# Windowed attention and an MLP on one core: the first block turned in 64-column halves, and the second product done plainly in place of seven half-size products

## The chip, the cores and the metric

The kernel runs on one core of a Trainium2 chip. A core has a matrix engine (TensorE, PE in the profile; its weight loads are PEld), a vector engine (VectorE, DVE), an activation engine (ScalarE, ACT), a general one (GpSimd, POOL) and a sync engine (SyncE, SP) that here only issues transfers. They run side by side, each through its own queue of instructions in order, and wait for each other by semaphores. The metric is the device time of one execution in microseconds. All arithmetic on PE is in 16-bit floats with 32-bit sums.

## The reference

Attention over a window of 128 tokens and 4 sink tokens, for 4 batches of 8 heads, 768 tokens and 64 numbers a head; its result, heads side by side (3072 tokens x 512), goes through an MLP.

```python
scores = scale * np.matmul(q, k.transpose(0, 1, 3, 2))
is_sink = pos[None, :] < int(n_sink)                    # n_sink = 4
rel = pos[:, None] - pos[None, :]
in_window = (rel >= 0) & (rel < int(window))            # window = 128
scores = np.where(is_sink | in_window, scores, -1000000000.0)
a = np.exp(scores - np.max(scores, axis=-1, keepdims=True))
a = a / (np.sum(a, axis=-1, keepdims=True) + 1e-09)
x = np.matmul(a, v)                                     # -> (3072, 512)
h = x @ w_in                                            # w_in 512 x 2048
g = h * (1.0 / (1.0 + np.exp(-1.702 * h)))
out = g @ w_out                                         # w_out 2048 x 512
```

## The kernel before

The tokens are cut into 12 blocks of 256, three to a batch. Each block goes through these stages:

- `load`: q, k and v come in as 32-bit floats by DMA. Blocks 0 to 3 bring q and k in two halves each, in rows of 2 KB (8 tokens of a head); later blocks bring them whole in shorter rows. They are cast to 16 bits (L295 is the helper `copy` that every cast and plain copy goes through): for block 0 on DVE or ACT, for block 1 on POOL, DVE or ACT, from block 2 on by POOL.
- `turn`: q and k are turned so that a head's 64 numbers lie across partitions (`blkT`). Blocks 0 to 3 are turned on PE (`turn_on_pe`, L541: four 128 x 128 products with a permutation matrix `perm` for each of q and k and each of two sets of tokens, and one or two copies out of PSUM); later ones by a transposing DMA (`turn_by_dma`, L563).
- `scores`: four head pairs a block; scores of a pair against the block and the block before it (L613), sinks (L593); in blocks 0 and 1 the mask is added by PE (L605), later it is multiplied in after the exponential by DVE (L645). ACT makes the exponentials (L638, L625).
- `back`: the attention product (L678), whose extra column gives the sum; its reciprocal (L696) and the normalisation, on DVE (L700) or, from block 3 on, ACT (L704); then a turn to `xT`, on PE for blocks 0 to 2 (L724), by DMA later (L712).
- `mm1`: the first MLP product, 64 products of 256 columns a block (L751), in eight groups; ACT makes a tanh of each group (L763) and DVE the gated activation `gT` (L765), since g is h(tanh(0.851 h) + 1)/2.
- the second product. Blocks 0, 1 and 11 do it plainly (`mm2`, L780): two groups of 16 products of 512 columns, each summed in a PSUM bank, halved and copied out by ACT (L797). Blocks 2 to 10 do it by `mm2_by_seven` (L870): a 2 x 2 split of tokens and of output and inner columns, with seven half-size products in place of eight: 56 products of 256 columns a block. For this DVE (or POOL) makes four forms of the weights once (`forms_of_w`, L825), DVE makes four sums and differences of the activations for each block (`forms_of_g`, L846, 144 instructions of 256 elements), ACT takes intermediate sums out of PSUM (L897, L900, L902) and DVE joins them (L903, L908). Three of the weight forms lie in the memory of the third load buffer (`third`).

PSUM has 8 banks. The order of all work is made before the kernel runs: `Plan.run` takes operations with their dependences, planned durations, priorities, the limits on banks ("o" is the class of the second product) and, for some, a choice of engines, and lays down one order for each engine's queue. So any change of an operation can move many others. The sizes of the rings of buffers stand in one line:

```python
RS, RQ, RV, RA, RX, RG, RTH, RO = 3, 2, 4, 4, 3, globals().get('OPT',{}).get('RG',3), 3, 2
```

RS counts the load buffers, RA the exponentials `at`, RG the activations `gT`, RO the output buffers (here two rows of 512 wide). Weights come by POOL's DMA queue (L376); the first waits for the last of block 1's four q and k loads. PE runs products with zeros (L982) while it has nothing to do at the start.

Of the kernel before, what the change touches and what calls it, by code (L numbers as in the profile page):

```python
# [14 lines left out]
P = 128  # L15
# [187 lines left out]
def kernel(  # L203
# [25 lines left out]
    KT, KX, AHEAD = globals().get('OPT',{}).get('KT',4), 3, globals().get('OPT',{}).get('AHEAD',0)  # L229
    RB, KM = 4, globals().get('OPT',{}).get('KM',2)  # L230
    RS, RQ, RV, RA, RX, RG, RTH, RO = 3, 2, 4, 4, 3, globals().get('OPT',{}).get('RG',3), 3, 2
    KS, LASTS = globals().get('OPT',{}).get('KS',2), globals().get('OPT',{}).get('LASTS',NK-1)
# [13 lines left out]
    perm = pool.tile([P, P], FP16, name="perm")  # L246
    dummy = pool.tile([P, 8], FP16, name="dummy")
# [7 lines left out]
    third = pool.tile([P, 3 * H * 2 * D], FP32, name="third")  # L255
    qk32 = ring("qk32", RS - 1, (P, 2, H, 2, D), FP32)
    v32 = ring("v32", RS - 1, (P, H, 2, D), FP32)
    qk32.append(third[:, 0 : 2 * H * 2 * D].rearrange("p (e h i d) -> p e h i d", e=2, h=H, i=2))
    v32.append(third[:, 2 * H * 2 * D :].rearrange("p (h i d) -> p h i d", h=H, i=2))
    wf = [third[:, 1024 * n : 1024 * n + 1024].bitcast(FP16).rearrange("p (s c) -> p s c", s=NS) for n in range(3)]  # L260
    wf += ring("wf", 1, (P, NS, d_model // 2), FP16)
    gF = ring("gF", 2, (P, NS, 3, P), FP16)
    part = pool.tile([P, 1024], FP32, name="part")
# [10 lines left out]
    osb = ring("osb", RO, (P, 2 * d_model), FP32)  # L274
    bank = [psp.tile([P, 512], FP32, name=f"bank{i}") for i in range(8)]

    OPT_ = globals().get("OPT", {}).get
    plan = Plan(8, {"m": 1, "s": 5, "t": 4, "a": 2, "x": 2, "h": RTH, "o": OPT_("NO", 3)})
# [32 lines left out]
    OPT = globals().get("OPT", {})  # L311
    VS_AT = NEVER + 14.505
# [17 lines left out]
    def masks():  # L330
# [9 lines left out]
        out=perm.rearrange("r (h g) -> r h g", h=NP), in_=ident.rearrange("r (g h) -> r h g", h=NP)),  # L340
        [o_ident], prio=NEVER, kind="const")

# [18 lines left out]
    OPT = globals().get("OPT", {})  # L361
    CAST_QK = ["DVE ACT", "POOL DVE"] + ["POOL"] * (NK - 2)
# [35 lines left out]

    o_cqk, o_cv, o_vs = {}, {}, {}
    o_qkT, o_ks, o_se, o_m, o_xT = {}, {}, {}, {}, {}  # L400

    def load(k):
        b, r = divmod(k, R)
        sl = k if k < RS else (k - 1) % (RS - 1)
# [5 lines left out]
        for e, src in enumerate((q, k_ap)):  # L410
            eng, dma = ("ACT", nc.scalar) if k == 0 and e else ("POOL", nc.gpsimd) if k == 2 else ("SP", nc.sync)
            lq[e] = []
            if k < KT:
# [28 lines left out]
        war = reuse("qk16", k % RQ)  # L442
        if k >= KT:
            C = slots(c16)
            for e in range(2):
                for j in range(2):
                    for i in range(2):
                        def f(eng, e=e, j=j, i=i):
                            copy(eng, C[64 * i : 64 * i + 64, e, :, j].rearrange("s p (h d) -> s p h d", h=2),
                                 dst[64 * j : 64 * j + 64, e, :, i].rearrange("s (p h) d -> s p h d", h=2))  # L450
                        o = plan.any(cast(512, CAST_QK[k]), f, lq[e] + war, prio=nominal(k - 1, -7), kind="cqk")
                        o_cqk[k, 2 * e + j, i] = o
        else:
# [8 lines left out]
        for o in {id(x): x for (kk, _, _), x in o_cqk.items() if kk == k}.values():  # L462
            uses("s32", sl, o)
# [41 lines left out]
    def turn(k):  # L505
# [7 lines left out]
        if k < KT:  # L513
# [5 lines left out]
        for p in range(NP):  # L519
            o_qkT[k, p] = [o[p] for o in o_t]  # L520
# [14 lines left out]

    def turn_on_pe(k, e, i, T, C, war):
        base = attend(k, 0) - 5 * L / 8

        def tp():
            for a in range(4):  # L540
                nc.tensor.transpose(f16(o_tp)[:, bass.ts(a, P)], C[:, a].rearrange("s h d -> s (h d)"), perm)  # L541

        o_tp = op("PE", 4 * pe_ns(P), 3 * pe_ns(P) + P / 2.4 + 166, tp, [o_cqk[k, e, 0], o_cqk[k, e, 1], o_perm],
# [112 lines left out]
    def back(k, p):  # L656
# [41 lines left out]
        def normal(eng):  # L698
            if eng == "DVE":
                nc.vector.tensor_tensor(out=X, in0=avp()[:, :, :, 0:D], in1=rc.to_broadcast((P, 2, 2, D)), op=ALU.mult)  # L700
                return
            for j in range(2):
                for i in range(2):
                    nc.scalar.activation(out=X[:, j, i], in_=avp()[:, j, i, 0:D], func=AF.Copy, scale=rc[:, j, i : i + 1])  # L704

        o_n = plan.any({"DVE": (340, 430), **({"ACT": (430, 550)} if OPT_("XA", 3) <= k else {})}, normal,
# [28 lines left out]
    o_g = {}  # L735

# [32 lines left out]
    def mm2(k):  # L769
        b, r = divmod(k, R)  # L770
        g = gT[k % RG]
        for j, c0, c1 in ((0, 0, 512), (1, 0, 512)) if k < NK - 1 else ((0, 0, 512), (1, 0, 384), (1, 384, 512)):
# [17 lines left out]
            if not c0:  # L790
                war = reuse("osb", (k % RO, j))
            O = osb[k % RO][:, bass.ts(j, d_model)]
# [12 lines left out]
            for i in range(2):  # L805
# [6 lines left out]
                uses("osb", (k % RO, j), o_d)  # L812

    def forms_of_w():

        W = w_out16.rearrange("p (s e) (h c) -> p s e h c", e=2, h=2)
        free = [o for (kk, _, _), o in o_cqk.items() if kk == 2] + [o for p in range(NP) for o in o_cv[2, p]]
        for j in range(4):
            x = slice(2 * j, 2 * j + 2)
            b11, b12, b21, b22 = (W[:, x, e, h] for e in range(2) for h in range(2))  # L820
            t1, t2, t3, t4 = (wf[n][:, x] for n in range(4))
            for n, (o_, a, b_, what) in enumerate(((t1, b12, b11, ALU.subtract), (t2, b22, t1, ALU.subtract),
                                                   (t3, b22, b12, ALU.subtract), (t4, b21, t2, ALU.subtract))):
                def f(eng, o_=o_, a=a, b_=b_, what=what):
                    (nc.gpsimd if eng == "POOL" else nc.vector).tensor_tensor(out=o_, in0=a, in1=b_, op=what)  # L825
                deps = [o_w[4 + j]] + ([o_wf[j, n - 1]] if n in (1, 3) else [])
                if n == 3:
                    deps.append(o_wf[j, 1])
                o_wf[j, n] = plan.any({"POOL": (1110, 1250), "DVE": (450, 550)}, f, deps + (free if n < 3 else []),
                                      prio=nominal(KS + 1, OPT_("WFP", -9) + j), kind="wf")  # L830

    def forms_of_g(k):

        g, F = gT[k % RG], gF[k % 2]
        G = g.rearrange("p (s e) (t q) -> p s (e t) q", e=2, t=2)
        war = reuse("gF", k % 2)
        w = OPT_("GW", 2)
        for s in range(0, NS, w):
            x = slice(s, s + w)
            a11, a21, a12, a22 = (G[:, x, n] for n in range(4))  # L840
            s1, s2, s4 = (F[:, x, n] for n in range(3))
            last = [o_g[k, i] for i in range(s, s + w)] + war
            four = []
            for o_, a, b_, what in ((s1, a21, a22, ALU.add), (s2, s1, a11, ALU.subtract), (a21, a11, a21, ALU.subtract), (s4, a12, s2, ALU.subtract)):
                def f(eng, o_=o_, a=a, b_=b_, what=what):
                    (nc.gpsimd if eng == "POOL" else nc.vector).tensor_tensor(out=o_, in0=a, in1=b_, op=what)  # L846
# [187 lines left out]
```

## Time and profile before

| | us |
|---|---|
| median of 3 runs | 223.22 (222.3 to 223.94) |
| the profiled execution | 222.3 |
| its span | 220.4 |
| PE busy | 209.2 (95%) |
| DVE busy | 177.0 (80%) |
| ACT busy | 135.7 (62%) |
| POOL busy | 93.3 (42%) |
| first MLP product starts | 18.98 |
| last product ends | 216.95 |

The span runs from the first to the last instruction; about 1.9 us lie around it. A product's booked time includes the way through the array, so that products overlap in the profile: how fast they go is read from one start to the next. The granted clock of PE is 1.0 throughout. A line of a group gives the line of the code, engine, operation, what is written from what, shapes, count, busy time and the mean of one in ns, and the idle time of the engine before it with what ended it. In a timeline the first two numbers are start and length in us.

### The profile page before, as it was taken

How to read it: one execution, taken by the hardware profiler on the slowest of the kernel's cores; microseconds unless marked ns; L12 is line 12 of the kernel's file. 1: busy time of each engine (PE TensorE's matmuls, PEld its weight loads, DVE VectorE, ACT ScalarE, POOL GpSimd, SP SyncE). 2: the span in 40 equal slices, each digit the busy share in tenths (PEclk: the TensorE clock that was granted, in tenths of full speed). 3: DMA queues.
4: the chain of work that ended last, by engine and by line, in shares of the span. 5: the costliest groups of instructions: out<-in, count | busy, mean ns of one | idle time of the engine just before them, and what ended most of it. 6: DMA issues, size and time to landing. Idle time of an engine off the chain costs nothing.

```text
span 220.4 us, 5881 instructions
## 1 busy us (share of the span) xinstructions
PE 209.2 (95%) x2282; PEld 164.8 (75%) x2282; DVE 177.0 (80%) x437; ACT 135.7 (62%) x298; POOL 93.3 (42%) x152
## 2 busy tenths in 40 slices
PE   7989999996998999999989999999999999999993
PEld 2447877574766887888878877888888988988852
DVE  3677855399999799889799999999799979875520
ACT  2697645877464777866845745866755656635420
POOL 2495440789995393076390492292840000000000
PEclk9999999999999999999999999999999999999999
DMA  5999999999457909695959939939746024024043
GB/s 192 340 235 205 207 302 234 302 308 287 110 111 143 265 24 190 173 218 104 303 141 194 261 72 175 261 85 236 234 94 147 0 51 100 0 51 95 0 97 97
DMA packets 65916, 36.60 MB, mean 166 GB/s; under 512 B 27968, under 2 KB 61120, under 8 KB 65888
## 3 DMA queue, kind: packets, MB, share of 16 engines
q1 hardware_dynamic: 60848, 30.19, 55.1%
q0 software_dynamic: 4592, 5.37, 12.8%
q10 hardware_dynamic: 448, 0.66, 0.9%
q8 instruction: 18, 0.29, 0.6%
q14 instruction: 10, 0.08, 0.1%
HBM read 27.56 MB, written 6.29 MB: 154 GB/s over the span
## 4 chain that ended last, share of the span: by engine, by line
PE 65%; DVE 24%; ACT 7%; issue 3%; DVEq 0%; ACTq 0%
PE bank L751 26%; PE bank L870 18%; DVE gT L765 7%; PE bank L780 6%; DVE gF L846 5%; PE bank L678 5%; PE bank L613 4%; ACT at L638 3%; PE bank L982 3%; DVE third L825 2%; DVE at L645 2%; DVE gT L846 2%; ACT th L763 2%; PE bank L605 1%; DVE osb L903 1%
## 5 line engine op out<-in xcount | busy, mean ns | idle before, releaser
L751 PE MATMUL bank<-xT,w_in 128*128 128x256 f16 x768 | 99.4, 273 | 0.2 <-DVE gT L765 0.2
L763 ACT ACTIVATE th<-bank 128x512 f16<-128x512 f32 x96 | 57.8, 604 | 49.1 <-PE bank L751 47.8
L751 PEld LDWEIGHTS <-w_in 128*128 128x128 f16 x768 | 72.7, 98 | 11.2 <-issue 1.8
L765 DVE SCALAR_TENSOR_TENSOR gT<-th,bank 128x512 f16<-128x512 f16 x96 | 65.2, 679 | 17.1 <-ACT th L763 16.4
L295 POOL CAST qk<-qk 64x512 f16<-64x512 f32 (+1 forms) x70 | 44.1, 633 | 39.7 <-DMA qk<-in_q_dram 29.1
L638 ACT ACTIVATE at<-bank 128x512 f16<-128x512 f32 (+1 forms) x96 | 49.1, 577 | 10.1 <-PE bank L613 10.1
L870 PE MATMUL bank<-third,gF 128*128 128x256 f16 x144 | 34.4, 273 | 1.4 <-DVE gF L846 1.4
L870 PE MATMUL bank<-w_out,gT 128*128 128x256 f16 x144 | 34.3, 273 | 0.0
L870 PEld LDWEIGHTS <-gT 128*128 128x128 f16 x288 | 27.7, 98 | 4.1 <-issue 0.9
L645 DVE TENSOR_TENSOR at<-at,bank 128x1024 f16<-128x1024 f16 (+1 forms) x40 | 25.2, 636 | 4.4 <-ACT at L638 4.4
L295 POOL CAST v<-v 64x512 f16<-64x512 f32 (+1 forms) x38 | 24.1, 636 | 2.8 <-PE bank L751 0.9
L870 PEld LDWEIGHTS <-gF 128*128 128x128 f16 x216 | 20.7, 98 | 4.7 <-DVE gF L846 1.9
L678 PE MATMUL bank<-v,at 128*128 128x65 f16 x352 | 21.1, 193 | 2.9 <-DVE at L645 2.4
L780 PE MATMUL bank<-w_out,gT 128*128 128x512 f16 (+2 forms) x112 | 23.6, 349 | 0.0
L678 PEld LDWEIGHTS <-at 128*128 128x128 f16 x352 | 17.1, 97 | 5.6 <-DVE at L645 4.3
L870 PE MATMUL bank<-wf,gT 128*128 128x256 f16 x72 | 17.2, 273 | 0.0
L870 PE MATMUL bank<-w_out,gF 128*128 128x256 f16 x72 | 17.1, 272 | 0.0
L780 PEld LDWEIGHTS <-gT 128*128 128x128 f16 x112 | 9.8, 98 | 7.0 <-issue 0.3
L678 PE MATMUL bank<-vs,ats 128*128 128x65 f16 x128 | 14.8, 193 | 0.0
L846 DVE TENSOR_TENSOR gF<-gF,gT 128x256 f16<-128x256 f16 x36 | 13.8, 382 | 0.8
L613 PEld LDWEIGHTS <-blkT 64*128 64x128 f16 x256 | 8.1, 94 | 8.0 <-issue 6.5
L704 ACT ACTIVATE xb<-bank,rcp 128x64 f16<-128x64 f32 x44 | 10.3, 323 | 5.5 <-DVE rcp L696 5.5
(67 smaller groups left out, 226.7 us busy)
## 6 DMA issues: line engine op xcount, KB each, us to landing
out_dram<-osb SPq DMA_DIRECT2D x46, 128.0 KB, 2.4
v<-in_v_dram SPq DMA_DIRECT2D x11, 512.0 KB, 6.6
qk<-in_q_dram SPq DMA_DIRECT2D x8, 512.0 KB, 4.9
qk<-in_k_dram SPq DMA_DIRECT2D x8, 512.0 KB, 6.1
w_in<-in_moe_w_in_dram POOLq DMA_DIRECT2D x4, 512.0 KB, 9.0
w_out<-in_moe_w_out_dram POOLq DMA_DIRECT2D x4, 512.0 KB, 12.4
qk<-in_q_dram SPq DMA_DIRECT2D x6, 256.0 KB, 5.1
qk<-in_k_dram SPq DMA_DIRECT2D x4, 256.0 KB, 5.2
```

The lines of the kernel that those rows point to most:

```text
L295: {"POOL": nc.gpsimd.tensor_copy, "DVE": nc.vector.tensor_copy, "ACT": nc.scalar.copy}[e](out=out, in_=in_)
L613: nc.tensor.matmul(f32(o_s, 2 * n + i)[:, c : c + w], src[d, j], Q[d].rearrange("d j s -> d (j s)")[:, q0 : q0 + w], start=k >= KM, stop=T ...
L638: nc.scalar.activation(out=A[:, i, 0:W], in_=f32(o_s, 2 * n + i)[:, 0:W], func=AF.Exp, scale=scale)
L645: nc.vector.tensor_tensor(out=A[:, :, 0:W], in0=A[:, :, 0:W], in1=mask(c0, c0 + W).unsqueeze(1).to_broadcast((P, 2, W)), op=ALU.mult,)
L678: nc.tensor.matmul(avp()[:, j, i], a_, v_, start=(n == 0), stop=(n == len(mms) - 1))
L704: nc.scalar.activation(out=X[:, j, i], in_=avp()[:, j, i, 0:D], func=AF.Copy, scale=rc[:, j, i : i + 1])
L751: nc.tensor.matmul(f32(holder[0])[:, bass.ts(e, TB)], w_in16[:, c, bass.ts(Fi, P)], X[:, c] if k < KX else X2[:, :, c], start=(c == 0), st ...
L763: o_t = op("ACT", 477, 600, lambda first=first: nc.scalar.activation(out=th[first.places[0]], in_=f32(first), func=AF.Tanh, scale=0.851), ...
L765: o_g[k, s] = op("DVE", 590, 700, lambda first=first, s=s: nc.vector.scalar_tensor_tensor(out=g[:, 2 * s : 2 * s + 2].rearrange("p a t -> ...
L780: nc.tensor.matmul(f32(holder[0])[:, 0:w], g[:, Fi, bass.ts(j, P)], w_out16[:, Fi, c0:c1], start=(Fi == 0), stop=(Fi == NF - 1),)
L846: (nc.gpsimd if eng == "POOL" else nc.vector).tensor_tensor(out=o_, in0=a, in1=b_, op=what)
L870: nc.tensor.matmul(f32(holder[0])[:, bass.ts(half, N)], lhs, rhs, start=fresh and s == 0 and half == what(0)[0][0], stop=s == NS - 1, skip ...
```

## The change

- Blocks 2 to 10 do the second product by `mm2`, as 0, 1 and 11 did. `mm2_by_seven`, `forms_of_w`, `forms_of_g` and their buffers are gone. The space goes to a third load buffer of its own, to six `at` and five `gT` in place of four and three; the output buffers are three of 512 in place of two of 1024. The second product may hold two banks at once, before three. The normalisation is always DVE's.
- Block 0 loads q and k by halves of head pairs: a half has heads 4y to 4y+3, one after the other, each as 32 rows of 2 KB (before: the even or the odd heads, with heads inside a group of tokens). Number, size and queue of the loads are the same. Each half is cast as it lies and turned by itself in `turn_halves`: for each of eight tokens of a row and each of the two heads of a pair one product of 64 columns into 64 partitions, 64 in all in place of 16 of 128 columns; then two copies. Head pairs 2y and 2y+1 depend on the halves y of q and k only.
- The other blocks that are turned on PE use a second matrix `perm8`, with the old order, which POOL makes after `perm`.
- The first weight load waits for the third of block 1's q and k loads in place of the fourth.

```diff
-    RS, RQ, RV, RA, RX, RG, RTH, RO = 3, 2, 4, 4, 3, globals().get('OPT',{}).get('RG',3), 3, 2
+    KN = globals().get('OPT',{}).get('KN',1)
+    RS, RQ, RV, RA, RX, RG, RTH, RO = 3, 2, 4, 6, 3, 5, 3, 3
...
-    plan = Plan(8, {"m": 1, "s": 5, "t": 4, "a": 2, "x": 2, "h": RTH, "o": OPT_("NO", 3)})
+    plan = Plan(8, {"m": 1, "s": 5, "t": 4, "a": 2, "x": 2, "h": RTH, "o": 2})
...
     o_perm = op("POOL", 330, 450, lambda: nc.gpsimd.tensor_copy(
-        out=perm.rearrange("r (h g) -> r h g", h=NP), in_=ident.rearrange("r (g h) -> r h g", h=NP)),
+        out=perm.rearrange("r (h p g) -> r h p g", h=2, p=2), in_=ident.rearrange("r (p h g) -> r h p g", p=2, h=2)),
         [o_ident], prio=NEVER, kind="const")
+    o_perm8 = op("POOL", 330, 450, lambda: nc.gpsimd.tensor_copy(
+        out=perm8.rearrange("r (h g) -> r h g", h=NP), in_=ident.rearrange("r (g h) -> r h g", h=NP)),
+        [o_ident], prio=NEVER+3, kind="const")
...
+            if k < KN:
+                for y in range(2):
+                    def f(e=e, y=y, src=src, dma=dma):
+                        to = halves(qk16[k % RQ])[:, e, y] if k in CD else dst[:, e].rearrange("s h i d -> s (h i d)")[:, 512 * y : 512 * y + 512]
+                        return dma.dma_start(to, src[b, 4 * y : 4 * y + 4, t0 : t0 + TB].rearrange("h (g i) d -> h g (i d)", i=8))
...
+        if k < KN:
+            for y in range(2):
+                two = [x for e in (1, 0) for x in turn_halves(k, e, y, T, halves(c16)[:, e, y], war)]
+                o_t.append(two)
+                for p in (2 * y, 2 * y + 1):
+                    o_qkT[k, p] = two
+        elif k < KT:
...
+    def turn_halves(k, e, y, T, C, war):
+        base = attend(k, 0) - 5 * L / 8 + 2 * y + e
+
+        def tp():
+            for i in range(8):
+                for h in range(2):
+                    d = slice(64 * h, 64 * h + 64)
+                    nc.tensor.matmul(
+                        f32(o_tp)[d, bass.ts(i, 64)], C[:, bass.ts(i, 64)], perm[:, d], start=True, stop=True,
+                    )
+
+        o_tp = op("PE", TPN, TPN + 170, tp, [o_cqk[k, e, y], o_perm], prio=base, acq=("t", 1), kind="tp")
...
-    def second(k):
-        if KS <= k < LASTS:
-            mm2_by_seven(k)
-        else:
-            mm2(k)
...
         if k_ >= 2:
-            second(k_ - 2)
+            mm2(k_ - 2)
...
-            g = o_first[OPT.get("WG", -1)]
+            g = o_first[OPT.get("WG", -2)]
```

## The prediction

> **What bounds the kernel now.** I read busy time by stretch first, because the shares over the whole span mix the start with the steady part. Columns: PE, PEld, DVE, ACT and POOL busy, clock, DMA share, GB/s.
>
> ```profile
> 20.00:50.00 30.00, 30.00 (x325) 21.70 (x324) 20.08 (x44) 18.75 (x35) 14.26 (x23) 1.00 1.12 266
> 50.00:180.00 130.00, 124.41 (x1428) 103.28 (x1424) 121.34 (x297) 85.08 (x195) 66.81 (x104) 1.00 0.69 163
> 180.00:210.00 30.00, 30.00 (x323) 26.56 (x316) 21.85 (x53) 17.25 (x36) 0.00 (x0) 1.00 0.19 45
> ```
>
> PE has no idle time from 20 to 50 us and from 180 to 210. Between them it idles 130.00 - 124.41 = 5.6 us, exactly where DVE is busy 121.34/130 = 93%. So PE's work sets the length, and the gaps in it are DVE's doing. The waits of PE say it by name:
>
> ```profile
> PE bank L678 <- DVE at L645: 2.4, 3, 1.7
> PE bank L593 <- DVE osb L903: 1.5, 3, 0.7
> PE bank L870 <- DVE gF L846: 1.4, 2, 1.0
> ```
>
> With 0.2 for L751 that is 5.5 us in nine waits. A 256-column matmul is booked for 273 ns, but the next starts 109 ns later, so a wait hides another 0.16: 5.5 + 9 x 0.16 = 7.0 us. What makes them is seen in the timeline at the largest:
>
> ```profile
> 50.33 1.12 DVE L825 TENSOR_TENSOR third<-w_out,third 128x512 f16<-128x512 f16 x1
> 51.37 1.37 DVE L825 TENSOR_TENSOR third<-w_out 128x512 f16<-128x512 f16 x1
> 52.66 0.28 DVE L295 COPY xT<-bank 128x256 f16<-128x256 f16 x1
> 52.86 0.54 DVE L645 TENSOR_TENSOR at<-at,bank 128x768 f16<-128x768 f16 x1
> ```
>
> Two weight forms (L825) stand 2.5 us on DVE ahead of the mask multiply (L645) that the attention product at 53.46 needs. The other two kinds are L846 and L903, DVE steps that exist only for the seven products.
>
> **Part 1, the second product, on the path.** A product of n columns costs its distance to the next start, read from the timeline of PE:
>
> ```profile
> 30.65 1.03 PE L780 MATMUL bank<-w_out,gT 128*128 128x512 f16 x4
> 31.52 1.91 PE L751 MATMUL bank<-xT,w_in 128*128 128x256 f16 x16
> ...
> 98.47 0.27 PE L870 MATMUL bank<-wf,gT 128*128 128x256 f16 x1
> 98.58 0.27 PE L870 MATMUL bank<-w_out,gT 128*128 128x256 f16 x1
> ```
>
> Four of 512 columns take 0.87 us, 217 ns each; 256 columns take 109. Out go 504 matmuls of 256 columns (144 + 144 + 72 + 72 + 72 in the groups), 55.0 us; in come 9 blocks x 32 of 512 columns, 288 x 0.216 = 62.2. Nothing hides this while PE is full: **+7.2 us**.
>
> **Part 2, the engines around it.** DVE loses 144 sums and differences of activations (13.8 + 13.1 + 12.8 + 12.5 = 52.2 us), 18 joins (6.2 + 6.1) and its 13 weight forms (8.7). It takes back 11 normalisations that ACT does now (44 pieces, 10.3 us), each 0.416: 4.6. So DVE goes from 177.0 to 177.0 - 73.2 + 4.6 = 108 us, half the span. ACT loses 12.2 (L897, L900, L902) and those 10.3, and gains 18 copies of 612 ns, 11.0: 135.7 to 124. POOL loses three forms, 3.6. DMA moves the same bytes, and SP's queue carries the same 48 stores and 17 transposes; two stores follow each copy now in place of four after both joins, so what stands behind them in that queue waits no longer than now. All this is beside PE; its worth is only what it does to the 7.0 us of waits. The bounds for these: all go (-7.0), or the same number returns (0). The stretches 20-50 and 180-210, with plain 512-column products or no attention, have DVE at 67-73% and no PE wait; that is the nearest row to a DVE at 50%, so I take nearly all: **-6.3 us**, leaving 0.7 for waits that a new order brings. What is late next: PE cannot lose its 0.1 us steps at changes of work (a score group's first weights, L613, wait 6.5 us in 19 places on "issue"), and those stay as they are. The wider rings (six at, five gT, third load buffers of their own) only take waits away; the plan of instructions holds two banks for the second product in place of three, with one ACT copy as release, and the product after next starts some 8 us later, so I cost it at nothing; were a copy held up by 1 us behind exponentials, it would still be covered.
>
> **Part 3, the start.** Until 18.98 us, where the first block's MLP begins, PE has long gaps and ACT has few:
>
> ```profile
> 7.08 1.56 ACT L295 COPY blkT<-bank 128x256 f16<-128x256 f16 x5 [3.50 <-PE bank L541]
> 9.18 2.50 ACT L638 ACTIVATE at<-bank 128x384 f16<-128x384 f32 x6 [0.54 <-PE bank L613]
> 11.70 1.25 ACT L295 CAST v<-v 64x256 f16<-64x256 f32 x3
> ...
> 14.43 1.88 ACT L295 CAST v<-v 64x512 f16<-64x512 f32 x3
> 16.33 1.09 ACT L638 ACTIVATE at<-bank 128x512 f16<-128x512 f32 x2
> ```
>
> From 9.18 ACT runs almost without a pause until the first tanh at 20.06. The four loads of block 0 keep their queues, their 2 KB rows and their count, so I let them land as now: casts at 4.39, 5.08, 6.12 and 6.79, the last done at 7.22. The gain on paper is that head pairs 0 and 1 need only the first two. But the instruction order of the changed kernel puts all 64 turning matmuls ahead of the first score, so pair 0 waits for the last cast anyway. Sixteen of them cost between 16 x 29 ns = 0.5 us (the attention product's 65 columns, 24 in 0.76) and 16 x 56 = 0.9 (the 128-column turn, 8 in 0.45); the lower is nearer in width. Turned by 7.8 (8.2), masks 0.34, scores 0.3: exponentials could start at 8.5 to 8.9, against 9.18. Then a step stands in ACT's queue that was on DVE: the cast of block 1's first K half.
>
> ```profile
> 8.84 0.43 DVE L295 CAST qk<-qk 128x512 f16<-128x512 f32 x1 [0.30 <-DMA qk<-in_k_dram]
> ```
>
> Its load lands at 8.84 and a cast of this size takes ACT 0.62: the first exponential starts at 9.46, 0.3 **later** than now, with eight exponentials, three V casts and the whole chain queued behind it. Later one V cast of 0.62 moves from ACT to POOL and a 0.3 copy of x comes to ACT: the two cancel. The second permutation (0.29 on POOL, after the first) and the earlier gate of the first weights (block 1's third load in place of its fourth, 0.7 us) lie in POOL's idle 1.8 us before its first cast and 1.0 before L376; uncovered, they would cost 0.3. Bounds of the start: +0.6 if ACT's lead stays lost, -1.0 if the better place of block 0's last two pairs in PE's queue (their attention product comes before two of block 1's score groups) reaches the first MLP product. I take **+0.1**.
>
> The page "TensorEngine Tiling (Array Packing)", section Feature Incompatibilities, speaks against the 64-wide turn: a matmul tiled by columns has no fast weight load. By the page "TensorE: Matmul & The Clock Gate", LDWEIGHTS, 64 columns then take 64/1.2 = 53 ns, so a step would be 0.85 us, an estimate; ACT's wait until 8.84 covers that too, and no row here shows a 64-column load.
>
> The tail (48 products from 209.84 to 216.95, then copies and stores to 220.4) stays.
>
> **Sum.** The profiled execution took 222.3 us (span 220.4 and 1.9 around it): 222.3 + 7.2 - 6.3 + 0.1 = 223.3. The median before is 223.22, 0.9 above that execution, and its runs spread over 1.6; I put this down to the DVE waits, which vary, so I carry none of it over: **223.3 us**, no change.
>
> **Rivals.** *Slower: ACT takes DVE's place as the one that PE waits for.* After a score group PE has about 2.2 us of other matmuls (by the order, 10 x 0.216) before the attention product that needs its exponentials and mask. The chain is 0.1 + two exponentials 1.1 + mask 0.68 + 0.1 = 2.0; if a tanh (0.60) is already running on ACT, 2.6, and PE waits 0.4. With two score groups in each of the eight blocks that look back at another, and 1 to 1.5 such waits a block, 8 to 12 x 0.4 = 3 to 5 us: 226.3 to 228. It decides from about six such places (+2.4). For it: ACT's share is 56% and its queue is in order; against it: the same distance of 2.2 us stands in most blocks now, and only three waits are on L645.
>
> *Faster: the start moves.* If block 0's MLP starts 1.0 us earlier and no wait is left, 222.3 + 7.2 - 7.0 - 1.0 = 221.5; with one step of 0.1 us less in each of the nine blocks (L870 waits 0.9 us on "issue" in 6 places), 220.6. For it: POOL and DVE are freer all along. Against it: ACT, which holds the start, is not.
>
> *The exchange does not pay at all:* waits stay because they come from the order and not from DVE's load: 222.3 + 7.2 = 229.5. Against it: L903 and L846 leave the kernel, and what held the mask at L645, L825, leaves too.
>
> **Chances.** About 1% (2.2 us) is what a measurement here can tell from no change, so the bounds are 221.0 and 225.4. Near balance 0.46 (221.0 to 225.4); ACT's waits 0.25 and no exchange 0.06, both slower, 0.31; start and small steps 0.23, faster. The range leaves out the 229.5 case, the upper part of ACT's and the best of the start: 220.7 to 227.0. Its likeliest case alone spans 221.7 to 225.0.
>
> **What will show it.** Part 1: one group of 368 matmuls of 512 columns at 216 ns spacing in place of the seven-product groups. Part 2: DVE busy near 108 us; no PE wait on L825, L846 or L903's successors; PE idle between 50 and 180 near 1 us. If PE waits for DVE at the mask or ACT appears as releaser, the rival holds. Part 3: first exponential at 9.4 to 9.5 after a cast that waits for DMA; first MLP product between 18 and 19.5. I would be wrong in kind if PE is idle over 3 us after 50 us, or if the first MLP product stands before 17.5.

## The result, and the profile after

| | before | after |
|---|---|---|
| median, same chip | 223.58 (222.3 to 224.03, 4 runs) | 232.78 (232.32 to 233.98, 4 runs) |
| ratio | | 1.0429 (95% interval 1.0369 to 1.049) |
| the profiled execution | 222.3 | 232.75 |
| span | 220.4 | 230.9 |
| last cast of block 0's q and k starts | 6.79 | 16.42 |
| first exponential | 9.18 | 18.96 |
| first MLP product | 18.98 | 29.04 |
| last product ends | 216.95 | 227.43 |

The changed kernel is 4.3% slower, 9.5 us above the prediction and 5.8 above the upper end of its range. The table says where: the first MLP product is 10.06 us late, the last one 10.48. Of the loss, 0.42 us lies in the 198 us between these two points, all the rest ahead of them. Some of the kernels below have single executions 2 to 4% above their others; medians are over all runs, ratios leave those runs out, and where a profile is of such an execution the text says so.

The stretches, with the columns as before (PE, PEld, DVE, ACT, POOL, clock, DMA share, GB/s). First the kernel before, where the later stretches stand in the prediction:

```profile
0.00:10.00 10.00, 8.80 (x51) 3.90 (x52) 4.62 (x16) 3.87 (x10) 3.17 (x10) 1.00 0.78 268
10.00:20.00 10.00, 9.04 (x130) 5.46 (x128) 7.58 (x26) 9.50 (x22) 9.07 (x17) 1.00 1.22 225
```

The changed kernel:

```profile
0.00:10.00 10.00, 4.98 (x13) 1.70 (x13) 1.30 (x8) 1.49 (x2) 2.26 (x8) 0.93 0.55 150
10.00:20.00 10.00, 4.80 (x78) 2.62 (x79) 3.26 (x8) 2.74 (x8) 2.52 (x4) 0.50 0.50 142
20.00:50.00 30.00, 29.15 (x311) 20.44 (x309) 19.44 (x47) 20.10 (x41) 15.12 (x26) 0.96 1.15 239
50.00:180.00 130.00, 130.00 (x1310) 88.46 (x1309) 79.09 (x168) 80.26 (x157) 68.15 (x115) 1.00 0.77 183
180.00:210.00 30.00, 30.00 (x283) 20.61 (x282) 16.76 (x34) 16.59 (x31) 0.00 (x0) 1.00 0.23 54
```

From 50 to 180 us PE has no idle time left, where before it had 5.6 us; DVE is at 79.09/130 = 61% in place of 93%. That is what the change of the second product was to do there. The loss is in the first two lines: from 10 to 20 us every engine is idle for more than half of the time, PE's clock is down at 0.50 (before 1.00), and the DMA share is 0.50 (before 1.22), at 142 GB/s in place of 225. So the kernel waits for data, though the DMA engines as a whole have time to spare.

The waits name the data. Columns: total, number of waits, longest.

```profile
DVE qk L288 <- DMA qk<-in_k_dram: 9.3, 3, 6.9
PE bank L569 <- DVE qk L288: 9.0, 3, 7.1
...
DVE qk L288 <- DMA qk<-in_q_dram: 4.9, 2, 3.6
```

But for one wait of 0.8 us in the first line, all of this is block 0: DVE waits for the loads of k and q, and PE's 64-column products (L569) wait for DVE's casts. In the timeline each of the four casts says that it waited for DMA:

```profile
8.76 0.43 DVE L288 CAST qk<-qk 128x512 f16<-128x512 f32 x1 [6.95 <-DMA qk<-in_k_dram]
12.78 0.43 DVE L288 CAST qk<-qk 128x512 f16<-128x512 f32 x1 [3.60 <-DMA qk<-in_q_dram]
...
14.74 0.43 DVE L288 CAST qk<-qk 128x512 f16<-128x512 f32 x1 [1.53 <-DMA qk<-in_k_dram]
...
16.42 0.43 DVE L288 CAST qk<-qk 128x512 f16<-128x512 f32 x1 [1.25 <-DMA qk<-in_q_dram]
```

Before:

```profile
4.39 0.43 DVE L295 CAST qk<-qk 128x512 f16<-128x512 f32 x1 [2.58 <-DMA qk<-in_k_dram]
...
5.08 0.43 DVE L295 CAST qk<-qk 128x512 f16<-128x512 f32 x1 [0.26 <-DMA qk<-in_q_dram]
...
6.12 0.43 DVE L295 CAST qk<-qk 128x512 f16<-128x512 f32 x1 [0.61 <-DMA qk<-in_k_dram]
...
6.79 0.43 DVE L295 CAST qk<-qk 128x512 f16<-128x512 f32 x1 [0.25 <-DMA qk<-in_q_dram]
```

Block 1's loads, whose order is unchanged and which follow in SP's queue, are late as well. The page gives KB each and the median us from issue to landing; of the loads in these two lines the trace has the landing of block 1's alone. Before, the lines read 5.1 and 5.2 us; after:

```profile
qk<-in_q_dram SPq DMA_DIRECT2D x6, 256.0 KB, 14.8
qk<-in_k_dram SPq DMA_DIRECT2D x4, 256.0 KB, 14.4
```

What the loads' packets do in between is counted from the trace's packet records. Before, 180 to 195 packets of 2 KB start in each of the three microseconds from 5 to 8, each takes 84 to 85 ns (the median), and the sum of their times is that of 16 to 17 engines. After, from 14 to 17 us, when almost no packets of another size are under way, 48 start in a microsecond and take 86 to 87 ns: 48 x 0.087 = 4.2 engines busy. The records do not name a packet's engine, so the number of engines is this sum; the DMA share from 14 to 16 us, 0.26 of 16, gives the same 4.2. A packet is as fast as ever; three quarters of the engines have nothing to do. The new source order is `h (g i) d -> h g (i d)`: 4 heads outermost, then 32 groups of rows. Before it was 32 groups, then 4 heads.

That the outermost count sets the number of engines is stated in the Trainium skill, page "DMA: Bandwidth & Descriptors", section "Why a DMA increments its semaphore by 16 and not by 1": the engines used are the largest number up to 16 that divides the slowest dimension of both sides, ignoring dimensions of size 1. With 4 heads against 128 partitions this is 4, and the 4.2 engines of this trace agree. The experiments test it.

### The profile page after: what moved, and what is told of

Read it like the earlier page. It is cut to its first block, busy times and chain, and to the rows that moved or that the text cites. A ratio compares the mean times of both kernels' runs of the same rounds, so it can differ in the third digit from the quotient of the medians.

```text
span 230.9 us, 5291 instructions
## 1 busy us (share of the span) xinstructions
PE 216.4 (94%) x2108; PEld 144.8 (63%) x2108; DVE 124.8 (54%) x271; ACT 127.0 (55%) x246; POOL 88.0 (38%) x151
## 4 chain that ended last, share of the span: by engine, by line
PE 88%; DMA 7%; DVE 1%; ACT 1%; SPq 1%; issue 0%
PE bank L795 37%; PE bank L824 35%; DMA qk<-in_q_dram 6%; PE bank L728 6%; PE bank L663 5%; PE bank L655 2%; PE bank L591 1%; DMA out_dram<-osb 1%; PE bank L643 1%; PE bank L767 1%; ACT v L288 1%; DVE xn L748 0%; SPq L418 0%; PE bank L569 0%; ACT osb L843 0%
## 5 line engine op out<-in xcount | busy, mean ns | idle before, releaser
L824 PE MATMUL bank<-w_out,gT 128*128 128x512 f16 (+2 forms) x400 | 99.8, 371 | 0.0
L688 ACT ACTIVATE at<-bank 128x512 f16<-128x512 f32 (+1 forms) x96 | 49.0, 571 | 10.8 <-PE bank L663 10.7
L288 POOL CAST v<-v 64x512 f16<-64x512 f32 (+1 forms) x43 | 26.0, 604 | 9.9 <-DMA v<-in_v_dram 7.7
L843 ACT ACTIVATE osb<-bank 128x512 f32<-128x512 f32 (+1 forms) x24 | 14.4, 600 | 11.0 <-PE bank L824 11.0
L748 DVE TENSOR_TENSOR xb<-bank,rcp 128x256 f16<-128x256 f32 x36 | 15.2, 421 | 0.7
L663 PE MATMUL bank<-blkT 64*128 64x256 f16 x192 | 13.9, 250 | 0.0
L728 PEld LDWEIGHTS <-ats 128*128 128x128 f16 x128 | 12.0, 97 | 2.1
L746 DVE RECIPROCAL rcp<-bank 128x4 f32<-128x4 f32 x48 | 8.5, 178 | 5.4 <-PE bank L728 5.0
L569 PE MATMUL bank<-perm,qk 128*64 128x64 f16 x64 | 2.3, 243 | 9.0 <-DVE qk L288 9.0
L288 DVE CAST qk<-qk 128x512 f16<-128x512 f32 x5 | 2.3, 452 | 14.1 <-DMA qk<-in_k_dram 9.3
L569 PEld LDWEIGHTS <-qk 128*64 128x64 f16 x64 | 1.9, 154 | 9.8 <-DVE qk L288 9.8
```

Of the source, the lines that this page charges most:

```text
L288: {"POOL": nc.gpsimd.tensor_copy, "DVE": nc.vector.tensor_copy, "ACT": nc.scalar.copy}[e](out=out, in_=in_)
L663: nc.tensor.matmul(f32(o_s, 2 * n + i)[:, c : c + w], src[d, j], Q[d].rearrange("d j s -> d (j s)")[:, q0 : q0 + w], start=k >= KM, stop=T ...
L688: nc.scalar.activation(out=A[:, i, 0:W], in_=f32(o_s, 2 * n + i)[:, 0:W], func=AF.Exp, scale=scale)
L728: nc.tensor.matmul(avp()[:, j, i], a_, v_, start=(n == 0), stop=(n == len(mms) - 1))
L746: o_r = op("DVE", 93, 190, lambda: nc.vector.reciprocal(out=rc, in_=avp()[:, :, :, D]), [o_a], prio=base - 1.2 * h8, kind="rcp")
L748: o_n = op("DVE", 340, 430, lambda: nc.vector.tensor_tensor(out=X, in0=avp()[:, :, :, 0:D], in1=rc.to_broadcast((P, 2, 2, D)), op=ALU.mult ...
```

## The experiments

Theory: block 0's loads run on 4 of 16 DMA engines, because 4 heads stand outermost in their source, and this is the whole loss at the start. Rival: the turn by 64-column products, or the exchange of the second product, costs it. A cause found on the way, the weights' first transfer, is tried from the sixth experiment on. "The old gate" below is that of the kernel before, where the first weight load waits for the fourth of block 1's q and k loads; "the earlier gate" is that of the changed kernel, which waits for the third.

**The groups outermost again.** The changed kernel with the same halves, the same four loads and the same turn; only the order in which a load walks its source, and with it the row order that `perm` puts right, is changed.

```diff
-    src[...].rearrange("h (g i) d -> h g (i d)", i=8)
+    src[...].rearrange("h (g i) d -> g h (i d)", i=8)
...
-    in_=ident.rearrange("r (p h g) -> r h p g", p=2, h=2)
+    in_=ident.rearrange("r (g p h) -> r h p g", p=2, h=2)
```

> The changed kernel with one thing undone: block 0's halves are read with the 32 row groups outermost and the four heads inside (partition 4g + head), and the permutation of block 0 is made to match. Theory A (a load whose source has the four heads outermost is carried by 4 of the 16 DMA engines): the loads land as in the kernel before, first cast at 4.4 us, last at 6.8, first MLP product at 18.9 to 19.6, span 220.2 to 222, time 222 to 224. Rival B (the late start comes from the load's place in the plan, from the queues or from the 64-column turn): the casts stay late or the turn costs, first MLP product at 25 us or later, time 229 to 233.

Measured: median 222.83 (222.11 to 230.0, 10 runs), ratio to the kernel before 0.9945 (0.9914 to 0.9976). The casts of block 0, with what DVE was idle for:

```profile
4.14 0.43 DVE L288 CAST qk<-qk 128x512 f16<-128x512 f32 x1 [2.33 <-DMA qk<-in_k_dram]
4.82 0.43 DVE L288 CAST qk<-qk 128x512 f16<-128x512 f32 x1 [0.25 <-DMA qk<-in_q_dram]
5.85 0.43 DVE L288 CAST qk<-qk 128x512 f16<-128x512 f32 x1 [0.61 <-DMA qk<-in_k_dram]
6.52 0.43 DVE L288 CAST qk<-qk 128x512 f16<-128x512 f32 x1 [0.24 <-DMA qk<-in_q_dram]
```

They stand 0.25 to 0.27 us earlier than before the change, the first MLP product is at 18.32, and 10 us are back. One permuted dimension was the whole loss; neither the 64-column turn nor the second product has a part in it.

**The plain second product alone.** The changed kernel with block 0 loaded and turned as before.

```diff
-    KN = globals().get('OPT',{}).get('KN',1)
+    KN = 0
```

> The changed kernel with block 0 loaded, cast and turned as before (even and odd heads, 128-column turns); only the plain second product, the rings and the earlier gate are left of the change. The exchange of the product alone: from the first MLP product to the last matmul 198 to 199 us against 198.0, first MLP product at 18.8 to 19.3, time 222 to 223.6, no clear difference from the kernel before. If the exchange itself costs (rival: waits that the late start hides), 225 or more.

Measured: median 222.25 (221.74 to 227.95, 10 runs), ratio 0.9947 (0.9908 to 0.9985). Parts 1 and 2 lose nothing. The profile is of the execution of 227.95 us and shows something else. From the first MLP product (24.61) to the last (222.60) it takes 197.99, as before; it only starts late. SP's issue of block 1's v, POOL's issue of the first weights, and the casts that wait for v:

```profile
8.89 1.49 POOL L374 DMA_DIRECT2D w_in<-in_moe_w_in_dram  x2 [0.31 <-DMA qk<-in_k_dram]
8.90 0.43 SPq L442 DMA_DIRECT2D v<-in_v_dram  x1
...
18.52 1.25 ACT L288 CAST v<-v 64x512 f16<-64x512 f32 x2 [4.34 <-DMA v<-in_v_dram]
18.52 0.43 DVE L288 CAST v<-v 64x512 f16<-64x512 f32 x1 [3.96 <-DMA v<-in_v_dram]
```

Issued at 8.90, this v is cast at 18.52; before it was issued at 8.89 and cast at 14.43. The packet records show what it stood beside: from 14 to 17 us 189 to 202 weight packets (1 KB, POOL's queue) start in each microsecond, and 9 of v (512 bytes, SP's queue). The earlier gate lets the weights be issued 10 ns ahead of this v; before they came 0.94 us after it. Coming first is not enough to hold v up, though: in the first experiment's profile, of an execution of 222.21 us, the weights are issued 0.06 us ahead of v, and its first cast is at 14.95. What decides it is not shown.

**The kernel before, with heads outermost.** The opposite test: nothing of the change but the order of block 0's source, and its turn with the plain identity.

```diff
-    src[b, h::2, t0 : t0 + TB].rearrange("p (g i) d -> g p (i d)", i=8)
+    src[b, h::2, t0 : t0 + TB].rearrange("p (g i) d -> p g (i d)" if k == 0 else "p (g i) d -> g p (i d)", i=8)
...
-    nc.tensor.transpose(f16(o_tp)[:, bass.ts(a, P)], C[:, a].rearrange("s h d -> s (h d)"), perm)
+    nc.tensor.transpose(f16(o_tp)[:, bass.ts(a, P)], C[:, a].rearrange("s h d -> s (h d)"), ident if k == 0 else perm)
```

> The kernel before with one thing added: block 0's four q and k loads are read with the four heads outermost, and its turn uses the identity in place of the permutation, so that the result is the same. Theory A: those loads pass at some 98 GB/s, last cast of block 0 at 15 to 17 us, first MLP product 9 to 10.5 us later than now, time 232 to 234. Rival C (the cast or the turn by halves of head pairs is what is late): nothing changes, 223 to 224.

Measured: median 235.23 (234.06 to 235.53, 4 runs), ratio 1.0516 (1.0453 to 1.0578). The casts of block 0 are at 8.59, 12.55, 14.53 and 16.25, within 0.25 us of those of the changed kernel, and the stretch from 14 to 16 us has DMA share 0.27, 4.3 of 16 engines:

```profile
14.00:16.00 2.00, 0.99 (x8) 0.77 (x8) 0.43 (x1) 0.34 (x2) 0.00 (x0) 0.50 0.27 100
```

The casts are where the theory had them; the first MLP product, at 30.97, is 12.0 us later than before where 9 to 10.5 were expected, and the time is 1.2 us above its range. The order of the loads alone makes the old kernel at least as slow as the new one.

**One head a load.** The changed kernel with each of the four loads cut in four of one head; a dimension of size 1 stands outermost then, and 32 groups behind it.

```diff
-    return dma.dma_start(to, src[b, 4 * y : 4 * y + 4, t0 : t0 + TB].rearrange("h (g i) d -> h g (i d)", i=8))
+    for z in range(0, 4, 1):
+        ins = dma.dma_start(to[32 * z : 32 * z + 32], src[b, 4 * y + z : 4 * y + z + 1, t0 : t0 + TB].rearrange("h (g i) d -> h g (i d)", i=8))
+    return ins
```

> The changed kernel with each half's load cut into four loads of one head each (32 rows of 2 KB, 64 KB in one stretch of memory): the order in memory stays head after head. Theory A: the outermost dimension is now 32, all 16 engines work; 16 issues of 0.6 us in place of 4 on the two queues cost 1 to 2.5 us, so first MLP product at 20 to 21.5, time 223.5 to 226. Rival D (reading one head's 64 KB stretch after another is slow in memory): the packets still come at some 98 GB/s, time 231 to 234.

Measured: 234.04 in one run. The time missed the expectation by 8 us, but the loads did what the theory says: block 0's casts are at 6.28, 6.62, 8.35 and 8.69. What came late was again block 1's v. Its issue, the weights', and the casts:

```profile
12.80 1.49 POOL L374 DMA_DIRECT2D w_in<-in_moe_w_in_dram  x2 [1.81 <-DMA qk<-in_k_dram]
13.15 0.70 SPq L444 DMA_DIRECT2D v<-in_v_dram  x1
...
25.00 0.62 ACT L288 CAST v<-v 64x512 f16<-64x512 f32 x1 [6.54 <-DMA v<-in_v_dram]
25.00 0.42 DVE L288 CAST v<-v 64x512 f16<-64x512 f32 x1 [6.51 <-DMA v<-in_v_dram]
25.04 0.86 POOL L288 CAST v<-v 64x512 f16<-64x512 f32 x1 [6.82 <-DMA v<-in_v_dram]
```

With 0.35 us of lead for the weights, v needs 11.9 us from issue to cast (before 5.5).

**Two heads a load.** If the outermost count is the number of engines, two heads must be slower than four. If it were the distance of the rows in memory, or the number of loads, they would not.

```diff
+    for z in range(0, 4, 2):
+        ins = dma.dma_start(to[32 * z : 32 * z + 64], src[b, 4 * y + z : 4 * y + z + 2, ...].rearrange("h (g i) d -> h g (i d)", i=8))
```

> The changed kernel with each of block 0's four loads split in two of two heads each (source walked as 2 heads x 32 groups x 2 KB). Theory (the outermost count of the source decides how many of the 16 DMA engines carry a load: 4 heads gave about 4 engines, 47 packets per us): two heads give 2 engines, about 24 packets per us, so the last cast of block 0 starts 25 to 28 us into the span (changed kernel 16.4) and the time is 241 to 246 us. Rival (it is the order in memory, rows of one head 8 KB apart in place of rows of a head pair, or the second permutation of the rows over partitions, that is slow): 47 packets per us as before the split, last cast 15 to 18, 231 to 235 us. Second rival (more loads in flight spread over more engines, which is why one head a load was fast): last cast 8 to 13, 223 to 230 us.

Measured: 253.02 in one run. Block 0's four casts (the timeline joins neighbours, so x2 is two casts; the last one starts at 28.53):

```profile
16.80 0.76 DVE L288 CAST qk<-qk 128x512 f16<-128x512 f32 x2 [14.99 <-DMA qk<-in_k_dram]
...
28.08 0.86 DVE L288 CAST qk<-qk 128x512 f16<-128x512 f32 x2 [10.53 <-DMA qk<-in_k_dram]
```

The packet records have 23 to 24 packets of 2 KB a microsecond from 8 to 12 us, at 87 ns: 2.1 engines. They come from SP's queue and ACT's at the same time, 12 and 12, so the loads of two queues do not take different engines; they share the same two. The theory holds in its rate; the last cast starts at 28.53, half a microsecond above its 25 to 28. Both rivals, which had 47 packets a microsecond or a last cast by 18 us, fall. The time is 7 us above the range: the first MLP product is at 48.37, 20 us after the last cast where it was 12 before, since the loads behind block 0's were late as well (block 1's v is issued at 30.43).

| heads outermost | packets of 2 KB a us | engines busy | last cast of block 0 |
|---|---|---|---|
| none (32 groups first) | 180 to 195 | 16 to 17 | 6.5 to 6.8 |
| 4 | 47 to 49 | 4.2 | 16.3 to 16.4 |
| 2 | 23 to 24 | 2.1 | 28.5 |

**One head a load, weights behind block 1's v.**

```diff
-            g = o_first[OPT.get("WG", -2)]
+            g = o_v1[0]
```

`o_v1` holds block 1's v load. 

> One head a load as before, and the first weight transfer now waits for block 1's v load in place of the third q/k load of block 1. Theory (the 234 us of one head a load were the v load of block 1 caught behind the weight transfers): v lands 1.5 to 3 us after its issue, the casts of block 1's v start by 17 us, first MLP product at 19 to 22, 223.5 to 227.5 us. Rival (one head a load is slow by itself, in the number of issues on the queue): first MLP product 28 or later, 232 us or more.

Measured: 228.62 in one run, between the theory's range and the rival's. Block 1's v, its issue and its first cast:

```profile
13.13 0.45 SPq L445 DMA_DIRECT2D v<-in_v_dram  x1
...
18.71 0.41 DVE L288 CAST v<-v 64x512 f16<-64x512 f32 x1
```

It lands at 17.88, 4.8 us after its issue, and is cast 5.6 us after it, as in the kernel before (5.5) and not after 11.9: v is no longer held up, but the theory had it land within 3 us and cast by 17. The first MLP product is at 26.61: the weights are now issued only at 19.07, PE's clock is at 0.50 from 14.3 to 21.2, and block 1's loads had been late before that, as each of the eight loads of block 0's q takes SP's queue some 0.4 us to issue. So of the 12 us above 222, 5.4 went with the gate; what is left is the price of more issues, later weights and the lower clock, which these runs do not tell apart.

**Groups outermost, weights gated as before.**

```diff
-            g = o_first[OPT.get("WG", -2)]
+            g = o_first[OPT.get("WG", -1)]
```

> The changed kernel with the groups outermost in block 0's loads (e1) and the first weight transfer gated on the fourth load of block 1, as in the kernel before, in place of the third. Theory (the runs of 227 to 230 us of e1 come from weight transfers that start before block 1's v load is through): median 222.0 to 222.7, at most one run of ten above 226. Rival (the gate has no part in it): two to four runs of ten above 226.

Measured: median 221.83 (221.58 to 222.77, 12 runs), ratio 0.996 (0.9934 to 0.9985). No run is above 222.8, where the earlier gate had four of ten above 226 (on another chip). The weights are issued at 9.64, the first exponential is at 9.15, the first MLP product at 17.97, and 198.40 us follow.

**Groups outermost, weights behind block 1's v.** The same edit as two above, on the kernel with the groups outermost.

> The changed kernel with the groups outermost in block 0's loads (e1) and the first weight transfer gated on block 1's v load. Theory: no run above 226; the weights start about 4 us later (13 in place of 9), and the median is between 222.2 (the weights were early enough) and 225 (the first MLP product waits for them). Rival (the gate has no part in the runs of 227 to 230): two or more runs of ten above 226.

Measured: median 223.88 (223.47 to 224.36, 12 runs), ratio 1.0042 (1.0022 to 1.0062). No run is late here either, but the first MLP product moves to 21.44: the weights, issued at 14.88, come too late. Of the three places only the old one has neither late runs nor late weights; by their ratios the earlier gate (0.9945) and the old one (0.996) do not differ beyond their intervals.

**The plain product alone, weights gated as before.** The second experiment with the one edit of the seventh.

> Parts 1 and 2 alone (e2: block 0 loaded and turned as before, plain second product), with the first weight transfer gated on the fourth load of block 1 as in the kernel before, in place of the third as in e2. Theory (parts 1 and 2 were sized rightly, +7.2 and -6.3 to -7 us, and the runs of 227 to 228 us of e2 came from the earlier gate): first MLP product at 18.7 to 19.3, 198.0 to 198.6 to the last matmul, median 222.0 to 223.0 us, at most one run of ten above 226. Rival (e2's gain of 1 us was that of the earlier gate): 223.0 to 224 us.

Measured: median 222.27 (221.83 to 223.18, 12 runs), ratio 0.9993 (0.9965 to 1.002). First MLP product at 19.00, before 18.98; 197.65 us follow, before 197.97. This is parts 1 and 2 without anything else: no change that can be measured. The 197.65 us lie a little below the expected 198.0 to 198.6. The two kernels with the earlier gate (the first and second experiment) had 6 of 20 runs above 226; this one and the seventh, with the old gate, none of 24. These counts are from different chips, and beside the first two the kernel before, with the old gate, had one run of 19 above 226 (226.08). So the gate is the likely cause of the late runs; a trace exists of one of the six alone.

**Seven products on the even blocks alone.** Three more kernels tried to get more out of the exchange. First, the kernel before with the seven products on five of the nine blocks (a second line asks the same for the sums and differences).

```diff
-        if KS <= k < LASTS:
+        if KS <= k < LASTS and (k) % 2 == 0:
```

> The kernel before, but only the even blocks of 2 to 10 (five of nine) have the second product by seven half-size products; the four odd ones take the plain product. Theory (the exchange of parts 1 and 2 nearly cancels because the DVE work of nine blocks makes TensorE wait about 7 us; the waits fall faster than the work when DVE is eased): 4 x 0.8 = 3.2 us more of TensorE's own work, waits of 7.0 us fall to 1 to 3.5 us, from the first MLP product to the last matmul 194.5 to 197 us (before 197.97, the plain product 198.4), time 220 to 222.3 us. Rival (the waits sit inside each block by seven, so they fall in proportion to 4 us): 197.5 to 198.5 between, 222.5 to 224 us.

Measured: median 223.94 (223.44 to 226.19, 12 runs), ratio 1.0078 (1.0043 to 1.0114); 198.88 us from the first MLP product to the last. The theory missed; the rival has the time right and the stretch by 0.4 us too short. Counted as distance between two starts beyond what the first one's columns usually take (109 ns for 256), where that is over 20 ns, PE's delays from 40 to 190 us are 11.8 us before, 9.5 here and 4.4 with the plain product. So 2.3 us of delays went, and 3.2 us of work (4 x 0.8) came in. Of what stays, 4.6 us lie between 50 and 70 us (before: 4.5), where the weight forms are made once, however many blocks use them.

**Part 3 alone, and both.** The kernel before with block 0 by halves, groups outermost, and all that `turn_halves` needs; and this with the even blocks.

```diff
+    KN = 1
...
+            if k < KN:
...
+                        return dma.dma_start(to, src[b, 4 * y : 4 * y + 4, t0 : t0 + TB].rearrange("h (g i) d -> g h (i d)", i=8))
```

> Part 3 alone, in the kernel before: block 0 by halves of head pairs and 64-column matmuls with the groups outermost in its loads, seven products kept, first weight transfer gated as before. Theory (the halves themselves start the work about 1 us earlier, 17.97 in place of 18.98 in e7, and the middle keeps its 198 us): first MLP product at 17.8 to 18.5, 221.8 to 222.9 us. Rival (the earlier start is lost again in the waits on DVE): 198.5 or more between first MLP product and last matmul, 223 to 224 us.

> Both edits: block 0 by halves with the groups outermost, seven products on the even blocks alone. Theory: the two gains add, 219.2 to 221.5 us, the fastest of all. Rival: no gain over the plain product with the groups outermost (221.8), 221.5 to 223 us.

Measured: 224.34 (220.35 to 225.85, 6 runs, five of them at 223.85 or more; the kernel before has 222.78 beside it) and 225.95 (224.89 to 226.36, 6 runs), ratio 1.0128 (1.0084 to 1.0173). Both expectations missed. The start is there (first MLP product at 18.44 and 18.31), but 201.08 and 202.28 us follow. One cause is visible in the stretches of the first of the two, whose profile is of an execution of 225.08 us, 2% above the fastest:

```profile
67.00:68.00 1.00, 0.31 (x3) 0.02 (x1) 1.00 (x3) 0.07 (x1) 0.88 (x3) 1.00 0.00 0
68.00:69.00 1.00, 0.21 (x2) 0.21 (x3) 0.97 (x3) 0.00 (x0) 0.94 (x2) 1.00 0.62 124
69.00:70.00 1.00, 0.40 (x4) 0.20 (x3) 1.00 (x3) 0.00 (x0) 0.88 (x2) 1.00 1.15 215
70.00:71.00 1.00, 0.95 (x17) 0.61 (x17) 1.00 (x7) 0.29 (x1) 0.00 (x0) 0.89 1.14 214
71.00:72.00 1.00, 1.00 (x6) 0.74 (x5) 0.39 (x3) 1.00 (x4) 0.00 (x0) 0.50 0.97 217
```

PE is busy for only 0.92 of three microseconds while DVE is full, and from 70.8 to 74.2 its clock is at 0.50 (0.89, 0.50, 0.50, 0.50 and 0.91 from 70 to 75 us): 1.7 us lost beside the wait itself. The longest wait there, 1.48 us, is of the half-size products for DVE's sums of activations. The second kernel has the same stretch (PE busy 0.89 us from 67 to 70, clock 0.50 from 70.0 to 73.5); the kernel before, whose clock stays at 1.00, has not. Why the other order of instructions brings it, and whether the run of 220.35 us went without it, stays open.

## Why the prediction was wrong

**The step that failed** is in part 3: "The four loads of block 0 keep their queues, their 2 KB rows and their count, so I let them land as now: casts at 4.39, 5.08, 6.12 and 6.79". They landed so that the casts began at 8.76, 12.78, 14.74 and 16.42. The step's own premise was true, and it was not enough: queue, row size and count do not say how many engines carry a load. The order of the dimensions does, and the diff shows it in one line, `h (g i) d -> h g (i d)`. The section on the change describes this line ("heads 4y to 4y+3, one after the other"), and the prediction priced it at nothing. With 512 rows of 2 KB in the four loads and 48 a microsecond, as measured since, the four would have needed 512/48 = 10.7 us in place of 512/180 = 2.8, and the sum would have been 8 us higher; the last cast came 9.6 us later. That other loads' packets pass through the same four engines fits the rest: from 11 to 13 us, while 512-byte packets of another load start, the 2 KB ones fall to 32 to 36 a microsecond. It was not tested.

No rival held this case either. All three were about engines on the path; none priced a transfer. "A transfer that takes longer" has a row in the profile of before, the landing times of 5.1 and 5.2 us for the loads of blocks 1 and 3, which the working never used.

**Part 1**, +7.2: right. In the changed kernel 368 products of 512 columns stand 216 ns apart, as said.

**Part 2**, -6.3: right in kind, a little small. Delays of PE from 50 to 180 us fell from 11.1 us to 4.0 (counted as above), and what stays are 42 steps of about 0.1 us, which were to stay. So all 7.1 us went, in place of 6.3 of 7.0. In sum, parts 1 and 2 were put at +0.9 and measured between -0.3 (the plain product alone, old gate) and +0.4 (the changed kernel). DVE's busy time was put at 108 us and is 124.8. The mistake is one of units: the page's 177.0 is time covered, while the 73.2 taken from it are sums of single durations, and neighbours overlap. The single durations on DVE sum to 201.4 us before and 133.6 after; the difference, 67.8, is close to the 73.2 - 4.6 = 68.6 of the prediction. It changed nothing, since DVE had room enough at either figure.

**Part 3, without the loads**, +0.1: the run with the groups outermost and the old gate shows what the halves are worth. The first exponential is at 9.15, expected at 9.46 and 9.18 before: it does stand behind ACT's cast of 0.62 us, as said, but that cast starts at 8.62 in place of 8.84. The first MLP product is 1.0 us earlier than before, which is the lower bound that the prediction gave and did not take; its reason is borne out, as the attention products of block 0's last two pairs start at 14.63 in place of 15.75 and 16.25. Not all of that 1.0 us is left in the time (0.4 by the medians 221.83 and 222.27, 0.7 by the ratios 0.996 and 0.9993), as 198.40 us follow in place of 197.65. Sixteen 64-column products were put at 0.5 to 0.9 us; at full clock 64 of them start within 1.0 us, so sixteen take 0.25. In that kernel they start in pairs, the two of a pair 0 to 3 ns apart and the next pair 31 ns later: the two of a pair, which write different halves of the partitions, run together. The estimate of 0.85 from the Trainium skill's page "TensorE: Matmul & The Clock Gate", LDWEIGHTS, 53 ns for a load of 64 columns, is not borne out: a pair of such loads starts every 32 ns, though a single one is booked at 113 ns, against 98 for a load of 128 columns.

**The earlier gate**, costed at nothing: wrong, as far as the runs tell. It lay in POOL's idle time, as said, but what it issues meets another transfer. The 0.3 us, "uncovered", counted POOL's time and not the 512 KB that a weight load moves. It goes with times 5 to 8 us longer in 6 of 20 runs; in the others a gain is not clear (ratios 0.9945 and 0.9947 against 0.996 and 0.9993 with the old gate, with intervals that overlap).

**The rival that ACT takes DVE's place** has no sign in the trace: PE has 130.00 us of work in the 130 us from 50 on. The rival that the exchange does not pay at all falls with the 7.1 us of part 2.

## What to carry to other kernels

When a diff changes the order of dimensions in a transfer, read the outermost size of both sides before anything else, and price the transfer by how many engines it can use: here 4 engines in place of 16, with equal bytes, rows and issues, moved the last cast from 6.8 to 16.4 us. A transfer that is issued earlier is not free because its issue is hidden: ask which smaller transfer it may overtake. And if both columns of a sum are taken from a profile, take both as covered time or both as sums of durations.

## What the runs showed of the hardware

- A load whose source has 4 or 2 heads outermost keeps 4.2 or 2.1 DMA engines busy, with unchanged packets of 84 to 87 ns, and two queues with such loads share the same engines (with 2 outermost, 12 and 12 packets a microsecond, 2.1 engines in all). The other engines stay free for others: from 6 to 9 us of the changed kernel 83 to 102 packets of 2 KB a microsecond start on SP's queue, block 1's among them, twice what four engines take.
- Where the weights' packets of 1 KB come first, a load of 512-byte packets on another queue can be held up, but not by one rule: in the second experiment its rest gets 9 starts a microsecond beside 189 to 202, in the fourth some 140 beside 140 once it has begun, and in the first, with the weights 0.06 us ahead, it is cast only 0.5 us later than before. In the kernel before and in the two with the plain product and the old gate, v's last packets start between 13 and 14 us and nothing of the kind is seen.
- After a stretch with PE almost idle its clock is at 0.50 and comes back only after some 4 to 5 us of full work: in part 3 alone PE is full from 70.05 us on and the clock is back at 74.2, after 3.4 us at 0.50; in the changed kernel the clock is at 0.50 from 8.7 to 22.3 us, and PE is full from 16.9 on. There it costs little, since PE waited for data anyway: the first exponential is 9.78 us late, the first MLP product 10.06.
